# Attention with chunk selection and a gated FFN: in batches 1 to 3, keys, queries with mask columns and attention output transposed by DMA, chunk extremes from a chunk-per-partition load

## The chip, the cores and the metric

The kernel runs on one core of a Trainium2 chip. The metric is the device time of one execution in microseconds (us); lower is better. The result of every run below was compared with the reference. A run counts as slow when it is over 1.5% above the fastest of its kernel. Three runs are slow by this rule, one each of c2_early (382.78 us), c3_all (367.29) and k3 (357.8); medians and ranges below are of fast runs alone. A ratio is the mean time of one kernel's fast runs over the mean time of the other's fast runs in the same rounds on the same chip, with a 95% interval, so it is not quite the ratio of the medians that are quoted beside it.

Engines are named as in the profile: PE is TensorE (matmuls, and transposes done as matmuls against an identity), DVE is VectorE, ACT is ScalarE, POOL is GpSimd, SP is SyncE, which here only issues DMA transfers. Each engine has its own list of instructions. For PE, ACT and DVE a scheduler picks the order of that list when the kernel is built; for POOL and SP, and in the opening, the order is that of the program. In the traces an instruction whose input is late holds back what stands behind it: in the changed kernel (after), DVE stood 2.61 us for a load in front of a reduction (which began at 126.25 us) and SyncE 4.9 us for its input in front of an output transpose (at 258.39), and neither began a later instruction in that time.

## The reference, cut to what matters

```
B, H, S, D = 4, 8, 768, 64;  chunk = 32;  nc = 24;  top_k = 6
k_min, k_max = min and max of each chunk of 32 keys            # "chunk extremes"
ub   = sum over d of max(q * k_min, q * k_max)                 # a bound per query and chunk
ub   = where(chunk is not in the query's future, ub, -1e9)
sel  = the 6 chunks with the largest ub of each query
p    = softmax over keys of (q @ k.T / 8) where sel and causal, else -1e9
x    = (p @ v), heads side by side: 3072 tokens x 512
out  = (sigmoid(x @ w_gate) * (x @ w_val)) @ w_out             # d_ff = 1536
```

## The kernel before

The work is cut into eight units, each half a batch of 384 queries: 0a, 0b, 1a, ... 3b. The first half of a batch is "a" and sees only the first 384 keys, the second is "b" and sees all. After an opening, the kernel runs in stages. A stage holds the attention of one unit, the FFN of the unit before it, the preparation (transposed keys and queries, bounds, picks) of the unit after it, and loads for the unit after that. The matmuls of the three are interleaved, so that PE always has something to do.

The mask costs no instruction of its own: the score matmul contracts over 96 rows, 64 of the head and 32 more. On the key side those 32 rows (of `headK`) hold a fixed pattern with a large negative number where the key lies in that chunk; on the query side (of `headQ`) they hold 1 for each chunk that was not picked.

The parts that change:

```
def keys_t(u, p, pool, tag="ps"):            # PE: three 128x128 transposes of f32 keys, two heads at a time
    ...
    for x in range(HB):
        nc.tensor.transpose(ps[:, x:T:HB], u.k[:, x, 2 * p:2 * p + 2, :].rearrange(...), ident32)
def extremes(u, p):                          # DVE: max and min over each chunk, from the transposed keys
    pv = u.kps[p].rearrange("p (c s) -> p c s", s=CH)
    for e, op in enumerate((ALU.max, ALU.min)):
        nc.vector.tensor_reduce(out=u.kmm[:, p, e, :], in_=pv, op=op, axis=AX.X)
def keys_f(u, p, eng):                       # ACT or DVE: cast to f16 into headK
    for e in range(2):
        eng(headK[u.b % 2][0:64, 2 * p + e, u.rows], ps[64 * e:64 * e + 64])
# queries_t, queries_f: the same for queries.  signs: relu(q), relu(-q), for the bounds
def pick(u, j):                              # bounds back to query rows, sixth largest, "not picked" flags
    ...
    nc.vector.tensor_tensor(apt[j][:, u.sel0:HB, :, 0:cb], ubm, mx[:, :, :, 5:6]..., ALU.is_lt)
def pick_t(u, j, eng):                       # PE: flags transposed; ACT or DVE: into headQ[64:96]
    ...
def turn(u, c):                              # attention output of two heads to xT, which the FFN reads
    ps = ppr.tile([128, T], F16, tag="ps", ...)
    for x in range(HB):
        nc.tensor.transpose(ps[:, 128 * x:128 * x + 128], u.x[:, x, 128 * c:128 * c + 128], ident16)
    nc.vector.tensor_copy(u.xT[:, c, :], ps)
def ffn_gv(u, fb):                           # 12 times a unit
    ... gp = four matmuls of wg16 with u.xT      # "g_" in the profile
    nc.scalar.activation(gate, gp, AF.Tanh, scale=0.5)
    ... vp = four matmuls of wv16 with u.xT      # "v_"
    nc.vector.scalar_tensor_tensor(hg, gate, 1.0, vp, ALU.add, ALU.mult)   # DVE must do this to free gp's and vp's space
```

The softmax here doesn't subtract the row's maximum and nothing guards it: scores larger than these inputs give would overflow.

Of the kernel before, what the change touches and what calls it, by code (L numbers as in the profile page):

```python
# [8 lines left out]
F32 = mybir.dt.float32  # L9
F16 = mybir.dt.float16  # L10
# [8 lines left out]
def kernel(  # L19
# [23 lines left out]
    consts = ctx.enter_context(tc.tile_pool(name="consts", bufs=1))  # L43
    keep = ctx.enter_context(tc.tile_pool(name="keep", bufs=1))
    loads = ctx.enter_context(tc.tile_pool(name="loads", bufs=2))
    nat = ctx.enter_context(tc.tile_pool(name="nat", bufs=1))
    sel = ctx.enter_context(tc.tile_pool(name="sel", bufs=1))
    ubp = ctx.enter_context(tc.tile_pool(name="ubp", bufs=2))
    attp = ctx.enter_context(tc.tile_pool(name="attp", bufs=4))
    small = ctx.enter_context(tc.tile_pool(name="small", bufs=3))  # L50
    xnatp = ctx.enter_context(tc.tile_pool(name="xnatp", bufs=2))
    xtp = ctx.enter_context(tc.tile_pool(name="xtp", bufs=2))
    gatep = ctx.enter_context(tc.tile_pool(name="gatep", bufs=3))
    hglp = ctx.enter_context(tc.tile_pool(name="hglp", bufs=18))
    outp = ctx.enter_context(tc.tile_pool(name="outp", bufs=3))
    PS = bass.MemoryType.PSUM
    pff = ctx.enter_context(tc.tile_pool(name="pff", bufs=3, space=PS))
    psc = ctx.enter_context(tc.tile_pool(name="psc", bufs=3, space=PS))
# [2 lines left out]
    class Unit:  # L61
        def __init__(self, b, half):
            self.b, self.half = b, half
            self.name = f"{b}{'ab'[half]}"
            self.qa, self.qb = HB * half, HB * half + HB
            self.rows = slice(T * half, T * half + T)
            self.sel0 = 1 - half
            self.m = HB - self.sel0
            self.paired = b == 0
            self.cb = T // CH * (half + 1)  # L70
            self.banks = HIGH if half else LOW
            self.where = {}
            base = 0
            for bk in self.banks:
                for (jb, i0, n) in bk:
                    for o in range(0, n, 128):
                        self.where[((i0 + o) // 128, jb)] = base + o
                    base += n
            self.width = base
            self.att, self.pv, self.kps, self.qps, self.ubT = {}, {}, {}, {}, {}  # L80

    LOW = [
# [8 lines left out]
    ]  # L91
    units = [Unit(b, half) for b in range(B) for half in range(2)]

    def load(u):
        for n, src in (("k", k), ("q", q)):
            t = loads.tile([128, H, HB, D], F32, tag="raw" + n, name=f"raw{n}_{u.name}")
            for j in range(2):
                nc.sync.dma_start(t[:, 4 * j:4 * j + 4], src[u.b, 4 * j:4 * j + 4, u.rows].rearrange(  # L98
                    "h (p x) d -> p h x d", x=HB))
            setattr(u, "raw" + n, t)  # L100
        u.v = loads.tile([128, HB, H, D], F32, tag="v", name=f"v_{u.name}")
        for i in range(HB):
            r = T * u.half + 128 * i
            nc.sync.dma_start(u.v[:, i], v[u.b, :, r:r + 128].rearrange("h p d -> p h d"))  # L104

    def regroup(u, n, parts):
        raw = getattr(u, "raw" + n)
        if not hasattr(u, n):
            setattr(u, n, nat.tile([128, HB, H, D], F32, tag=n, name=f"{n}_{u.name}"))
        t = getattr(u, n)  # L110
        for f, h0, h1 in parts:
            f(t[:, :, h0:h1, :], raw[:, h0:h1].rearrange("p h x d -> p x h d"))  # L112
# [3 lines left out]
    epat = consts.tile([32, NC, CH], F16, tag="epat")  # L116
    NQ = 2 * HB - 1
    pen = consts.tile([128, NQ, NC], F32, tag="pen")
    kmx = keep.tile([128, NP, 2, 32], F32, tag="kmx", name="kmx")
    kcat, v16s, apt, headK, headQ = [], [], [], [], []  # L120
    for i in range(2):
        kcat.append(keep.tile([128, H, 32], F32, tag=f"kcat{i}", name=f"kcat{i}"))
        headK.append(keep.tile([96, H, S], F16, tag=f"hk{i}", name=f"hk{i}"))
        headQ.append(keep.tile([96, H, T], F16, tag=f"hq{i}", name=f"hq{i}"))
        apt.append(keep.tile([128, HB, 4, 32], F16, tag=f"ap{i}", name=f"ap{i}"))
        v16s.append(keep.tile([128, 2 * HB, H, D + 1], F16, tag=f"v16{i}", name=f"v16{i}"))

# [4 lines left out]
    def constants():  # L132
        make_identity(nc, ident32)
        nc.vector.memset(epat, 0.0)
        nc.gpsimd.affine_select(
            out=epat, in_=epat, compare_op=ALU.not_equal, fill=NEG,
            base=0, pattern=[[-1, NC], [0, CH]], channel_multiplier=1,
        )
        fill_pattern(0, nc.sync)
        nc.vector.memset(kmx, 0.0)  # L140
        nc.vector.memset(pen, 0.0)
        nc.gpsimd.affine_select(
            out=pen, in_=pen, compare_op=ALU.is_ge, fill=-1e9,
            base=128, pattern=[[128, NQ], [-CH, NC]], channel_multiplier=1,
        )
        for i in range(2):
            nc.vector.memset(kcat[i], 0.0)
            nc.vector.memset(apt[i], 0.0)
            nc.gpsimd.memset(v16s[i][:, :, :, D:D + 1], 1.0)
        nc.vector.memset(headQ[0][64:96, :, 0:128], 0.0)  # L150
        nc.vector.tensor_copy(ident16, ident32)

    wg16 = keep.tile([128, 4, D_FF], F16, tag="wg16")
    wv16 = keep.tile([128, 4, D_FF], F16, tag="wv16")
# [13 lines left out]
    def cast_v(u):  # L168
        nc.gpsimd.tensor_copy(v16s[u.b % 2][:, u.qa:u.qb, :, 0:D], u.v)  # L169
# [63 lines left out]
    def queries_f(u, p, eng):  # L233
        ps = u.qps.pop(p)
        for e in range(2):
            eng(headQ[u.half][0:64, 2 * p + e, :], ps[64 * e:64 * e + 64])  # L236

    def bounds(u, j):
        s0 = 128 * u.sel0
        n = T - s0  # L240
        ps = ppr.tile([128, T], F32, tag="ps", name=f"ubT_{u.name}_{j}")
        for i, e in [(i, e) for e in range(2) for i in range(4)] if u.paired else []:
            h, r = 4 * j + i, 64 * (i % 2)
            nc.tensor.matmul(ps[32 * i:32 * i + 32, 0:n], kmx[r:r + 64, h // 2, e, :],
                             u.qs[r:r + 64, h - h % 2 + e, s0:T], start=(e == 0), stop=(e == 1))
        for i in [] if u.paired else range(4):
            nc.tensor.matmul(ps[32 * i:32 * i + 32, 0:n], kcat[u.b % 2][:, 4 * j + i, :],
                             u.qs[:, 4 * j + i, s0:T], start=True, stop=True)
        t = ubp.tile([128, T], F32, tag="ubT", name=f"ubTs_{u.name}_{j}")
        nc.scalar.copy(t[:, 0:n], ps[:, 0:n])  # L250
        u.ubT[j] = t

    def pick(u, j):
# [10 lines left out]
        for x in range(m):  # L264
            for h in range(4):
                nc.vector.max(mx[:, x, h, :], ubm[:, x, h, :])
        nc.vector.tensor_tensor(apt[j][:, u.sel0:HB, :, 0:cb], ubm,  # L267
                                mx[:, :, :, 5:6].to_broadcast([128, m, 4, cb]), ALU.is_lt)

    def pick_t(u, j, eng):  # L270
        ps = ppr.tile([128, T], F16, tag="ps", name=f"apT_{u.name}_{j}")
# [7 lines left out]
    def score(u, h, x, pool=None, tag="ps"):  # L279
# [6 lines left out]
        o = 0  # L286
        for (jb, i0, w) in u.banks[x]:
            i = i0 - T * u.half
            nc.tensor.matmul(ps[:, o:o + w], headK[u.b % 2][:, h, 128 * jb:128 * jb + 128],  # L289
                             headQ[u.half][:, h, i:i + w], start=True, stop=True)  # L290
            o += w
        nc.scalar.activation(at[:, b0:b0 + n], ps, AF.Exp, scale=scale)  # L292
        if x == 0:
# [4 lines left out]
    def values(u, h):  # L298
        p, e = h // 2, h % 2
        if h == 0:  # L300
            u.x = xnatp.tile([128, HB, H * D], F16, tag="xnat", name=f"xnat_{u.name}")
        if e == 0:
            u.pv[p] = psc.tile([128, 2, HB, D + 1], F32, tag="ps", name=f"pv_{u.name}_{p}")
        at = u.att.pop(h)
# [6 lines left out]
        if e == 1:  # L311
            rz = small.tile([128, 2, HB], F32, tag="rz", name=f"rz_{u.name}_{p}")
            nc.vector.reciprocal(rz, ps[:, :, :, D])  # L313
            o = u.x[:, :, 128 * p:128 * p + 128].rearrange("p a (e d) -> p e a d", e=2)
            nc.vector.tensor_tensor(o, ps[:, :, :, 0:D], rz.unsqueeze(3).to_broadcast([128, 2, HB, D]), ALU.mult)

    def turn(u, c):
        if c == 0:
            u.xT = xtp.tile([128, 4, T], F16, tag="xT", name=f"xT_{u.name}")
        ps = ppr.tile([128, T], F16, tag="ps", name=f"xps_{u.name}_{c}")  # L320
        for x in range(HB):
            nc.tensor.transpose(ps[:, 128 * x:128 * x + 128], u.x[:, x, 128 * c:128 * c + 128], ident16)
        nc.vector.tensor_copy(u.xT[:, c, :], ps)

    hgl = {}
# [29 lines left out]

    A, V, G = nc.scalar.copy, nc.vector.tensor_copy, nc.gpsimd.tensor_copy

    def prep_tasks(u):
        even = [A, V, A, V] if u.half == 0 else [A, A, A, V]
        kf = [V, V, V, V] if u.half == 0 else [A, A, A, A]  # L360
        qf = [A, V, A, V]
# [16 lines left out]
    def opening(u, w):  # L378
# [77 lines left out]
        cast_v(w)  # L456
        for j in range(3):
            load_wo(j)
        fill_pattern(1, nc.sync)
        f = ffn_tasks(u)  # L460

        def more():
            f.pop(0)[1]()
# [73 lines left out]

    with tc.manual_schedule():
        prev = opening(units[0], units[1])
    load(units[2])  # L540
    for i in range(1, len(units)):
        u = units[i]
        prep = prep_tasks(units[i + 1]) if i + 1 < len(units) else []
        a = attend_tasks(u, prep)
        if i + 2 < len(units):
            a.insert(len(a) // 2, (0.0, lambda i=i: load(units[i + 2])))
        merge(a, prev)
        prev = ffn_tasks(u)
    for c, t in prev:
# [31 lines left out]
```

## Time and profile before

The first runs gave 357.35 us, median of 3 (355.92 to 360.1). The page of the profile, its heading, its part 1 (busy us, share of the span, instructions) and two rows of its part 2 (the span in 40 slices: clock granted to PE and mean DMA busy share, in tenths, 9 is 90% or more):

```profile
span 353.9 us, 7200 instructions
PE 316.5 (89%) x2736; PEld 197.0 (56%) x2736; DVE 216.4 (61%) x642; ACT 234.4 (66%) x501; POOL 74.1 (21%) x106
...
PEclk9979999999999999999999999999999999999999
DMA  8999992057900066001740039001100020001002
```

The DMA engines are 80% busy or more in the first 53 us (six slices of 8.8 us) and more than half idle on average after that. The stages, in the windows view of before (columns: window and length in us, then busy us and instruction count of PE, PEld, DVE, ACT and POOL, the clock granted, the DMA share, GB/s):

```profile
87.00:129.00 42.00, 38.91 (x318) 23.26 (x316) 27.59 (x86) 32.05 (x71) 9.63 (x13) 1.00 0.31 83
129.00:171.00 42.00, 39.90 (x387) 25.77 (x386) 28.82 (x84) 29.47 (x64) 7.74 (x12) 1.00 0.29 76
171.00:211.00 40.00, 36.82 (x296) 22.39 (x297) 26.95 (x80) 29.14 (x63) 9.27 (x12) 1.00 0.31 81
```

So PE works 37 to 40 of every 40 to 42 us: the middle stages are bound by the amount of work on PE, and DVE is idle for a third of the time. PE's waits are small. The longest ones, in the waits view of before (engine, instruction and its line, what it waited for; us in total, times, longest us):

```profile
PE kT_0a_172 L179 <- DVE k_0a L112: 4.9, 1, 4.9
PE v_0b_1593 L336 <- ACT gate_0b_1559 L333: 1.4, 1, 1.4
```

The first is in the opening, before there is anything to do. From then on nothing costs more than 1.4 us. The chunk extremes are short instructions on the 384 columns of one pair of heads, as a line of the groups view of before shows (busy us, mean ns of one | idle before and releaser):

```profile
L186 DVE TENSOR_REDUCE kmm_2a<-kT_2a_1933 128x12 f32<-128x384 f32 x2 | 1.1, 553 | 1.0 <-PE kT_2a_1933 L179 1.0
```

| before | us |
|---|---|
| span of the profiled execution | 353.9 |
| PE busy | 316.5 |
| PE not busy (span less busy) | 37.4 |
| DVE / ACT busy | 216.4 / 234.4 |
| the first 55 us, in which PE was busy 37 | 55 |

### The profile page before, as it was taken

The numbers are of one execution on the slowest core, as the hardware profiler recorded it, in microseconds if no ns is written. First come the engines' busy times: TensorE is split into PE (matmuls) and PEld (weight loads), VectorE is DVE, ScalarE is ACT, GpSimd is POOL, SyncE is SP. The second block draws the span as 40 slices with busy tenths as digits, with TensorE's granted clock in tenths as the row PEclk, the third lists the DMA queues.
The fourth block names the chain that finished last, engine by engine and source line by source line (L and its number), as shares of the span: only waits on it lengthen the run. The fifth ranks groups of instructions, "written<-read, shape, count | busy, mean of one in ns | idle before, by whom it ended". The sixth has DMA issues, their size and how long they took to land.

```text
span 353.9 us, 7200 instructions
## 1 busy us (share of the span) xinstructions
PE 316.5 (89%) x2736; PEld 197.0 (56%) x2736; DVE 216.4 (61%) x642; ACT 234.4 (66%) x501; POOL 74.1 (21%) x106
## 2 busy tenths in 40 slices
PE   4678687999988999999987999999998999999995
PEld 3265345656554566655664466665665456665552
DVE  6576548985667569864776469883585574322430
ACT  4683467787888475876789375884789467665321
POOL 3393204211420040210421032201421011110000
PEclk9979999999999999999999999999999999999999
DMA  8999992057900066001740039001100020001002
GB/s 223 268 207 224 232 226 49 0 163 198 267 3 0 31 199 130 2 0 62 222 77 0 32 113 215 3 0 52 41 0 2 0 87 4 2 3 59 31 0 89
DMA packets 50642, 31.13 MB, mean 88 GB/s; under 512 B 26032, under 2 KB 47536, under 8 KB 50608
## 3 DMA queue, kind: packets, MB, share of 16 engines
q1 hardware_dynamic: 45856, 25.96, 28.2%
q0 software_dynamic: 4752, 4.72, 7.8%
q8 instruction: 21, 0.34, 0.4%
q14 instruction: 13, 0.11, 0.1%
HBM read 28.31 MB, written 6.29 MB: 98 GB/s over the span
## 4 chain that ended last, share of the span: by engine, by line
PE 54%; ACT 16%; issue 10%; DVE 8%; DMA 5%; SPq 4%; POOL 2%; ACTq 0%; POOLq 0%; DVEq 0%
DMA v_0b<-in_v_dram 5%; SPq L104 2%; ACT hq_117 L236 2%; SPq L98 1%; ACT hq_112 L236 1%; ACT qs_2b L227 1%; ACT qs_3b L227 1%; ACT qs_1b L227 1%; ACT hk_116 L198 1%; PE o_2b_4225 L345 1%; PE o_1b_2989 L345 1%; PE o_1a_2399 L345 1%; ACT qs_1a L227 1%; PE o_2a_3645 L345 1%; PE o_0b_1743 L345 1%
## 5 line engine op out<-in xcount | busy, mean ns | idle before, releaser
L336 PEld LDWEIGHTS <-wv_121 128*128 128x128 f16 x384 | 37.0, 97 | 38.4 <-issue 16.6
L330 PEld LDWEIGHTS <-wg_120 128*128 128x128 f16 x384 | 35.2, 98 | 16.1 <-issue 1.9
L289 PEld LDWEIGHTS <-hk_111 96*128 96x128 f16 x240 | 19.7, 101 | 13.0 <-issue 8.2
L289 PEld LDWEIGHTS <-hk_116 96*128 96x128 f16 x240 | 19.2, 97 | 9.4 <-issue 3.1
L179 PE MATMUL kT_0a_172<-ident_105,k_0a 128*128 128x128 f32 x3 | 0.9, 430 | 4.9 <-DVE k_0a L112 4.9
L295 POOL TENSOR_SCALAR_AFFINE_SELECT att_0b_776<-att_0b_776 128x384 f16<-128x384 f16 x1 | 0.5, 515 | 19.7 <-ACT att_0b_776 L292 19.7
L179 PEld LDWEIGHTS kT_0a_172<-ident_105,k_0a 128*128 128x128 f32 x3 | 0.5, 213 | 4.8 <-issue 4.8
L277 ACT COPY hq_117<-apT_0b_735 32x384 f16<-32x384 f16 x4 | 1.9, 469 | 1.8 <-PE apT_0b_735 L273 1.8
L112 ACT COPY k_0a<-rawk_0a 128x384 f32<-128x384 f32 x2 | 1.0, 512 | 2.9 <-DMA rawk_0a<-in_k_dram 2.9
L192 DVE TENSOR_SCALAR kcat_110<-kmm_2b 64x24 f32<-64x24 f32 x8 | 2.8, 350 | 0.1
L192 DVE TENSOR_SCALAR kcat_115<-kmm_3b 64x24 f32<-64x24 f32 x8 | 2.8, 350 | 0.1
L313 DVE RECIPROCAL rz_3b_4888<-pv_3b_4849 128x6 f32<-128x6 f32 x1 | 0.2, 196 | 4.3 <-PE pv_3b_4849 L309 4.3
L277 DVE COPY hq_112<-apT_3a_3801 32x256 f16<-32x256 f16 x4 | 1.2, 288 | 2.7 <-PE apT_3a_3801 L273 2.7
L277 DVE COPY hq_112<-apT_2a_2555 32x256 f16<-32x256 f16 x4 | 1.2, 288 | 2.7 <-PE apT_2a_2555 L273 2.7
L169 POOL CAST v_114<-v_0b 128x1536 f16<-128x1536 f32 x1 | 1.5, 1465 | 6.1 <-DMA v_0b<-in_v_dram 6.1
L313 DVE RECIPROCAL rz_1b_2434<-pv_1b_2339 128x6 f32<-128x6 f32 x1 | 0.2, 196 | 4.0 <-PE pv_1b_2339 L309 4.0
L313 DVE RECIPROCAL rz_2b_3680<-pv_2b_3585 128x6 f32<-128x6 f32 x1 | 0.2, 197 | 4.0 <-PE pv_2b_3585 L309 4.0
L273 PEld LDWEIGHTS <-ap_118 128*128 128x128 f16 x20 | 1.7, 98 | 1.5 <-DVE ap_118 L267 0.2
L162 POOL DMA_DIRECT2D wg_120<-in_moe_w_gate_dram x3 | 2.4, 808 | 0.0
L348 ACT ACTIVATE osb_3b_5093<-o_3b_5080 128x512 f32<-128x512 f32 x1 | 0.6, 597 | 2.8 <-PE o_3b_5080 L345 2.8
L198 ACT CAST hk_111<-kT_0b_494 64x384 f16<-64x384 f32 x2 | 0.9, 474 | 2.2 <-DVE kmx L186 2.2
L169 POOL CAST v_114<-v_0a 128x1536 f16<-128x1536 f32 x1 | 1.5, 1469 | 4.4 <-DMA v_0a<-in_v_dram 4.4
(1976 smaller groups left out, 1085.3 us busy)
## 6 DMA issues: line engine op xcount, KB each, us to landing
wg_120<-in_moe_w_gate_dram POOLq DMA_DIRECT2D x3, 512.0 KB, 8.9
wv_121<-in_moe_w_val_dram POOLq DMA_DIRECT2D x3, 512.0 KB, 12.0
wo_122<-in_moe_w_out_dram POOLq DMA_DIRECT2D x3, 512.0 KB, 13.6
rawk_0a<-in_k_dram SPq DMA_DIRECT2D x2, 384.0 KB, 3.8
rawq_0a<-in_q_dram SPq DMA_DIRECT2D x2, 384.0 KB, 5.2
v_0a<-in_v_dram SPq DMA_DIRECT2D x3, 256.0 KB, 6.3
rawk_0b<-in_k_dram SPq DMA_DIRECT2D x2, 384.0 KB, 6.3
rawq_0b<-in_q_dram SPq DMA_DIRECT2D x2, 384.0 KB, 6.5
```

The source lines that it names most:

```text
L98: nc.sync.dma_start(t[:, 4 * j:4 * j + 4], src[u.b, 4 * j:4 * j + 4, u.rows].rearrange("h (p x) d -> p h x d", x=HB))
L104: nc.sync.dma_start(u.v[:, i], v[u.b, :, r:r + 128].rearrange("h p d -> p h d"))
L169: nc.gpsimd.tensor_copy(v16s[u.b % 2][:, u.qa:u.qb, :, 0:D], u.v)
L192: nc.vector.tensor_scalar_mul(kcat[u.b % 2][64 * i:64 * i + 64, 4 * j + e:4 * j + 4:2, c0:c0 + T // CH], u.kmm[64 * e:64 * e + 64, 2 * j:2 ...
L198: eng(headK[u.b % 2][0:64, 2 * p + e, u.rows], ps[64 * e:64 * e + 64])
L227: nc.scalar.activation(o, src, AF.Relu, scale=sign)
L236: eng(headQ[u.half][0:64, 2 * p + e, :], ps[64 * e:64 * e + 64])
L277: eng(headQ[u.half][64:96, 4 * j + i, s0:T], ps[32 * i:32 * i + 32, s0:T])
L289: nc.tensor.matmul(ps[:, o:o + w], headK[u.b % 2][:, h, 128 * jb:128 * jb + 128], headQ[u.half][:, h, i:i + w], start=True, stop=True)
L330: nc.tensor.matmul(gp, wg16[:, c, 128 * fb:128 * fb + 128], u.xT[:, c, :], start=(c == 0), stop=(c == 3))
L336: nc.tensor.matmul(vp, wv16[:, c, 128 * fb:128 * fb + 128], u.xT[:, c, :], start=(c == 0), stop=(c == 3))
L345: nc.tensor.matmul(op, hgl[(u.name, fc)][:, 128 * tb:128 * tb + 128], wo16[:, fc, :], start=(fc == 0), stop=(fc == NFB - 1))
```

## The change

The intent is to take layout work off PE, ACT and DVE, and to give it to DMA engines that are half idle. For batches 1 to 3 ("wide" units), POOL casts keys and queries to f16, and transfers that are transposed on their way write them (`dma_start_transpose`, in the profile DMA_TRANSPOSE): keys together with their pattern rows (3 transfers of 256 KB a unit), queries together with their mask columns (6 of 128 KB), attention output (4 of 96 KB). Chunk extremes need f32 keys with a chunk's 32 keys in one partition's row, so the keys of a batch are loaded a second time in that shape (two loads of 768 KB) and DVE reduces over them; a reduction now covers 96 chunks (four heads) and 32 of the 64 head columns. A few buffers are taken away to make room. The diff, cut to its core:

```diff
-    attp = ... bufs=4      hglp = ... bufs=18     outp = ... bufs=3     v in `loads`, bufs=2
+    attp = ... bufs=3      hglp = ... bufs=15     outp = ... bufs=2     v in `loadv`, bufs=1
+            self.wide = b > 0
+    def load_span(u, j):                       # the second load of the keys
+        t = kcp.tile([96, CH, D], F32, tag="kc", ...)                       # bufs=1
+        nc.sync.dma_start(t, k[u.b, 4 * j:4 * j + 4].rearrange("h (c s) d -> (h c) s d", s=CH))
+    def keys_wide(u):
+        nc.gpsimd.tensor_copy(kn16[u.half][:, :, :, 0:D], u.k)
+        for x in range(HB):
+            r = T * u.half + 128 * x
+            nc.sync.dma_start_transpose(headK[u.b % 2][:, :, r:r + 128],
+                                        kn16[u.half][:, x].rearrange("p h c -> p (h c)"))
+    def span_reduce(u, j, e):
+        src = u.kc[j].rearrange("p s d -> p d s")
+        for d0 in (0, 32):
+            nc.vector.tensor_reduce(out=u.kmm[:, e, d0:d0 + 32], in_=src[:, d0:d0 + 32],
+                                    op=(ALU.max, ALU.min)[e], axis=AX.X)
+    def span_t(u, j):                          # one PE transpose of 96 columns, for four heads
+        nc.tensor.transpose(ps, u.kmm..., ident32[0:96, 0:96])
+    def queries_wide(u):
+        nc.gpsimd.tensor_copy(qn16[:, :, :, 0:D], u.q)
+        if u.sel0: ... first_rows(u, 0)        # the first 128 queries need no picks
+    def send_rows(u, j, x):
+        nc.sync.dma_start_transpose(headQ[u.half][:, 4 * j:4 * j + 4, 128 * x:128 * x + 128],
+                                    qn16[:, x, 4 * j:4 * j + 4].rearrange("p h c -> p (h c)"))
     def pick(u, j):
-        nc.vector.tensor_tensor(apt[j][:, u.sel0:HB, :, 0:cb], ubm,
+        dst = qn16[:, u.sel0:HB, 4 * j:4 * j + 4, 64:64 + cb] if u.wide else apt[j][...]
+        nc.vector.tensor_tensor(dst, ubm,
+        if u.wide:
+            for x in range(u.sel0, HB):
+                send_rows(u, j, x)
     def turn(u, c):
+        if u is not units[0] and not (u is units[-1] and c == 3):
+            nc.sync.dma_start_transpose(u.xT[:, c, :].rearrange("p (x i) -> p x i", x=HB),
+                                        u.x[:, c].rearrange("p x d -> p (x d)"))
+            return
... (prep_wide orders these tasks; loads of a later unit are spread over the stage;
     one fill of the key pattern is dropped from the opening)
```

Queries are still transposed on PE in f32 for the bounds, and their positive and negative parts are still made by ACT.

## The prediction

It was made before the changed kernel ran, and is quoted word for word, apart from two passages that are cut, with the cuts marked: a time for one transpose by DMA that no run of this case had measured, and the reason for the upper end of the range, which rested on a speed of the transposes that no trace had shown. The sum: 357 - 15 - 8 + 13 - 2 = 345 us. Two figures in it are estimates and more loosely based than the rest: 1.1 us for a reduction of 1024 elements (0.55 us for 384 columns would in proportion give 1.47), and 3 us of queue for the second key load, for which no measured number is given. The 18 and 14 us of queue are estimates from the 2.05 us that a v load of 256 KB occupied it for in before.

> **What bounds the kernel now.** The page: span 353.9 us, PE busy 316.5 (89%), ACT 234.4 (66%), DVE 216.4 (61%), POOL 74.1. The windows view splits it: the opening (0 to 55 us) is a chain of loads and small steps with PE busy 37 of 55; from 55 us each half batch is a stage of about 40 us, with PE busy 38.9 of 42 (87 to 129), 39.9 of 42 (129 to 171), 36.8 of 40 (171 to 211), DVE 27 to 29 and ACT 29 to 32. The chain of waits is 54% PE, 16% ACT, 8% DVE. So six middle stages are bound by PE's own work, with 2 to 3 us of scattered idle behind ACT (waits of 0.5 to 1.4 us).
>
> **What the change removes, per stage of batches 1 to 3.**
> - PE: 12 key transposes (start to start about 0.11 us, not the 0.27 us of one record), 4 query transposes in the first half only, 4 to 6 mask and 12 output transposes at about 0.055 us: 2.6 us together, 15 over six stages.
> - ACT, over all six: 24 key casts and 24 query casts of 0.474 us, 24 mask copies of 0.36 or 0.47 us, against 12 more sign activations of 0.376: net about 28 us.
> - DVE: 48 extremes of 0.55, 48 chunk scalings, 48 casts of 0.55, 24 mask copies, 27 output copies of 0.35; it gains 24 reductions of 96x1024 elements, near 1.1 us (estimate from 0.55 for 384 columns). Net about 55 us less.
>
> **What it adds.** All on the SyncE queue: per stage 3 key transposes of 256 KB, 4 to 6 query ones of 128 KB, 4 output ones of 96 KB, key and query loads cut to 256-byte pieces (v: 256 KB each, queue occupied about 2.05 us each in steady state, 6 to 7.5 us to landing), and every batch's keys a second time (1.5 MB). Loads are then about 9 x 2 = 18 us per stage plus some 3 for the second key load; if a transposed 256 KB costs like a 256 KB v load, transposes add about 14: an estimated 35 of 40 us of queue. [...] Latency is exposed at stage ends: the last picks come about 6 us before the next scores, and two batches of mask transposes plus the last output transpose queue behind each other. I expect 2 to 3 us of PE idle per boundary, waiting for query or output transposes. The opening loses one pattern fill.
>
> **Sum.** -15 us PE work, about -8 us of idle behind ACT and DVE, +13 us new waits, about -2 us in the opening: 345 us. Range 326 to 378 [...]. Faster by over 2%: 0.57; within: 0.22; slower: 0.21.
>
> **What would show it.** PE busy about 300 us or less; ACT near 205, DVE near 160; DMA share in the middle slices up from 0.3 towards 0.7 or more; key, query-mask and output transposes landing in 3 to 6 us; first PE waits of each stage naming DMA transposes; stages of 37 to 39 us.
>
> **What would make it wrong.** Transposes that take 6 us or more each, or SyncE held by a waiting transpose so that loads and output stores come late; DVE standing at the second key load.

## More of the kernel before

PE is busy 89% of the time, and its clock is full from the fourth slice on.

`gp` and `vp` live in three shared buffers of PE's accumulator memory. If DVE does not consume them, PE runs out of buffers after a block and a half.

## The result, and the profile after

The changed kernel took 402.04 us, median of 4 runs (400.39 to 404.97), against 357.26 us (355.92 to 360.1) for the kernel before in the same rounds. The ratio is 1.125 (1.1151 to 1.1349): slower by an eighth. The result is correct. The page of after, the same lines:

```profile
span 398.7 us, 6796 instructions
PE 324.7 (81%) x2547; PEld 195.7 (49%) x2547; DVE 180.3 (45%) x472; ACT 207.9 (52%) x441; POOL 79.5 (20%) x116
...
PEclk9867999996889696979978999696999999899999
DMA  8999990598439846796255956494437015001002
```

PE has 189 instructions fewer and is busy 8 us longer. ACT has lost 27 us and DVE 36 us, as intended. Neither helped. The new thing is the clock row: in the middle of the run it drops to 6 to 8 tenths again and again. The windows view of after:

```profile
154.00:202.00 48.00, 42.28 (x366) 26.57 (x364) 21.22 (x52) 28.24 (x62) 7.47 (x12) 0.89 0.67 124
202.00:247.00 45.00, 36.81 (x276) 21.55 (x277) 22.39 (x56) 22.83 (x49) 10.29 (x14) 0.92 0.70 132
247.00:298.00 51.00, 42.00 (x347) 25.79 (x347) 21.22 (x52) 27.13 (x59) 7.08 (x12) 0.87 0.57 119
298.00:335.00 37.00, 33.68 (x274) 20.44 (x271) 15.35 (x52) 22.08 (x49) 8.07 (x12) 1.00 0.37 73
```

The first two windows do the work of the last two shown of before: 48 us in place of 42, and 45 in place of 40. The DMA share more than doubled, and is still 0.3 or more short of full. The last window (the attention of 3a) is the only one of the four at full clock, and it takes 37 us; no extremes are prepared in it, and few transfers are left (DMA share 0.37). This is what the change gives where nothing stands still for long.

PE's waits, in the waits view of after:

```profile
PE xps_0a L415 <- DVE xT_0a L416: 5.9, 1, 5.9
PE kmT_1a L295 <- DVE kmm_1a L290: 5.2, 1, 5.2
...
PE v_0b L429 <- DVE hg_0b L432: 4.0, 1, 4.0
PE g_1b L423 <- DMA xT_1b<-xnat_1b: 3.9, 1, 3.9
PE g_2a L423 <- DMA xT_2a<-xnat_2a: 3.6, 1, 3.6
...
PE g_3a L423 <- DMA xT_3a<-xnat_3a: 3.1, 1, 3.1
```

The long ones are of two kinds. One ends with DVE: extremes (kmm), output copies and gates (hg) that come late. The other ends with a DMA: the transposed attention output (xT, 12.1 us in sum) and, in shorter pieces, the transposed queries (hq, 7.2 us). Summed over the whole waits view, PE waits 31.7 us for DVE (9.8 in before), 15.8 for ACT (22.1 in before) and 19.3 for DMA transfers (none in before).

**The first kind.** The groups view of after shows the reductions, and the timeline of DVE shows what one batch of them does:

```profile
L290 DVE TENSOR_REDUCE kmm_2a<-kc_2a 96x32 f32<-96x1024 f32 x8 | 14.8, 1866 | 4.5 <-DMA kc_2a<-in_k_dram 4.5
```

```profile
126.25 1.88 DVE L290 TENSOR_REDUCE kmm_2a<-kc_2a 96x32 f32<-96x1024 f32 x1 [2.61 <-DMA kc_2a<-in_k_dram]
128.06 0.18 DVE L402 RECIPROCAL rz_1a<-pv_1a 128x6 f32<-128x6 f32 x1
128.16 1.81 DVE L290 TENSOR_REDUCE kmm_2a<-kc_2a 96x32 f32<-96x1024 f32 x1
129.90 0.54 DVE L404 TENSOR_TENSOR xnat_1a<-pv_1a,rz_1a 128x384 f16<-128x384 f32 x1
130.36 1.00 DVE L432 SCALAR_TENSOR_TENSOR hg_0b<-gate_0b,v_0b 128x384 f16<-128x384 f16 x2
```

The columns of a timeline are start, length, engine, line, operation, tiles, and in brackets the idle time before it and its releaser. DVE stood 2.61 us for the second load of the keys, then did two reductions of 1.8 to 1.9 us, and reached the gates (hg_0b) only at 130.36. By then PE had used up its buffers: the wait of 4.0 us for hg_0b in the list above ends at 130.95. DVE is 45% busy, but what it does is in the way of what PE needs.

**The second kind.** The timeline of SyncE's queue in after, around the wait of g_2a:

```profile
238.53 3.81 SPq L311 DMA_TRANSPOSE hq<-qn  x3
242.44 0.53 SPq L443 DMA_DIRECT2D out_dram<-osb_1b  x1
243.08 3.84 SPq L311 DMA_TRANSPOSE hq<-qn  x3
247.01 1.00 SPq L443 DMA_DIRECT2D out_dram<-osb_1b  x1
248.11 1.20 SPq L410 DMA_TRANSPOSE xT_2a<-xnat_2a  x1
```

and DVE's and PE's timelines at the same place, the output tile that the last transpose reads, and the first matmul that waits for it:

```profile
242.43 0.56 DVE L404 TENSOR_TENSOR xnat_2a<-pv_2a,rz_2a 128x384 f16<-128x384 f32 x1
...
250.46 0.48 PE L423 MATMUL g_2a<-xT_2a,wg 128*128 128x384 f16 x1 [3.56 <-DMA xT_2a<-xnat_2a]
```

The output was ready at 242.99 (242.43 + 0.56) and its transpose was issued at 248.11, 5.1 us later, and the matmul started 2.35 us after that. In between SyncE was occupied by three query transposes of 1.28 us each and a store of 1.0 us. The number of bytes hardly matters for this time: in the whole run the median occupation of SyncE was 1.20 us for 96 KB, 1.26 us for 128 KB and 1.33 us for 256 KB (9 of the 81 took 1.6 to 2.8), against 0.33 us for the shortest store of an output block. The times to landing, in the list of DMA issues of after (queue, kind, count, KB each where they are given, median us from issue to landing), were all short:

```profile
rawk_2a<-in_k_dram SPq DMA_DIRECT2D x3, 256.0 KB, 8.0
rawq_2a<-in_q_dram SPq DMA_DIRECT2D x3, 256.0 KB, 4.6
...
hq<-qn SPq DMA_TRANSPOSE x36, 2.5
...
hk<-kn SPq DMA_TRANSPOSE x18, 3.3
```

A transposed 256 KB (hk) landed in 3.3 us, plain loads of 256 KB in 4.6 (rawq_2a) and 8.0 (rawk_2a). In this trace no group of transposes landed later in the median (3.4 us at most, xT_0b) than such a load (4.1 us at least, rawq_3b). It is no test of transposing alone, since the loads read DRAM tensors (in_k_dram, in_q_dram) and the transposes read tiles.

SyncE also stood still at output transposes whose input was not ready: 4.0 us before 214.30 and 4.9 us before 258.39. The second key load was issued right behind each (215.5 and 259.6). This was a danger that the prediction had named. It is not what made DVE wait for these loads, though: in a3_turn_pe below, which has no such transposes, DVE still stood for them, 4.6 us for kc_2a and 7.1 for kc_3a (4.5 and 4.1 in after).

**The clock.** After a wait PE does not go on as before. The windows view of after, around the wait of 3.9 us for xT_1b, in steps of 2 us:

```profile
204.00:206.00 2.00, 0.00 (x0) 0.00 (x0) 0.00 (x0) 0.34 (x1) 2.00 (x3) 0.81 0.26 49
206.00:208.00 2.00, 0.51 (x2) 0.25 (x2) 0.00 (x0) 0.00 (x0) 1.31 (x2) 0.50 0.32 64
...
210.00:212.00 2.00, 2.00 (x7) 0.88 (x6) 0.56 (x1) 1.02 (x3) 0.00 (x0) 0.50 0.72 139
212.00:214.00 2.00, 2.00 (x18) 1.28 (x17) 0.99 (x3) 1.24 (x3) 0.52 (x1) 0.98 0.00 0
```

PE is idle from 203.6 to 207.5. From 206 to 212 it has half its clock. At half clock it gets 7 instructions done from 210 to 212, at full clock 18 from 212 to 214. The mean of 0.81 from 204 to 206 puts the fall at about 205.2, only 1.6 us after PE had stopped, and windows of 0.5 us put the rise at 212.1: 6.8 us at half clock, about 4.5 us of them with work. In such windows after has twelve stretches at half clock, ten of 6.8 us and two of 3.4 (14.1 to 17.5 and 338.4 to 341.8 us), 75 us in all; before has one of 6.8 us in the opening (21.5 to 28.3) and half clock in its last 1.3 us, after PE's last matmul. Elsewhere in after the clock fell after single waits of 2.6 us (one ends at 173.8, the other at 269.5). A wait of this size was not always enough: in q1_merge, below, waits of 2.6 and 2.1 us between 254 and 260 left the clock full. What else decides it is not shown.

**The sum.** The difference in span can be split exactly, by definition, into three: idle time of PE (span less busy time), time lost to the lower clock, and the rest, PE's work at full clock. The second is an estimate from the trace: for each window of 1 us, PE's busy time times the missing part of the clock. It assumes that all of PE's work slows with the clock.

| us, profiled executions | before | after | difference |
|---|---|---|---|
| span | 353.9 | 398.7 | +44.8 |
| PE not busy | 37.4 | 73.9 | +36.5 |
| lost to half clock | 3.2 | 29.7 | +26.5 |
| PE work at full clock | 313.3 | 295.1 | -18.2 |

This is bookkeeping. It says where PE's time is, and not yet what caused it.

### The profile page after: what moved, and what is told of

It reads as the page before. It is cut to its first block, busy times and chain, and to the rows that moved or that the text cites. A ratio compares the mean times of both kernels' runs of the same rounds, so it can differ in the third digit from the quotient of the medians.

```text
span 398.7 us, 6796 instructions
## 1 busy us (share of the span) xinstructions
PE 324.7 (81%) x2547; PEld 195.7 (49%) x2547; DVE 180.3 (45%) x472; ACT 207.9 (52%) x441; POOL 79.5 (20%) x116
## 5 line engine op out<-in xcount | busy, mean ns | idle before, releaser
L429 PEld LDWEIGHTS <-wv 128*128 128x128 f16 x384 | 39.9, 104 | 55.8 <-issue 34.9
L378 PEld LDWEIGHTS <-hk 96*128 96x128 f16 x480 | 41.3, 105 | 33.5 <-issue 23.2
L423 PEld LDWEIGHTS <-wg 128*128 128x128 f16 x384 | 37.1, 103 | 25.8 <-issue 12.4
L381 ACT ACTIVATE att_1b<-sc_1b 128x512 f16<-128x512 f32 (+1 forms) x32 | 16.9, 574 | 7.4 <-PE sc_1b L378 7.2
L381 ACT ACTIVATE att_2b<-sc_2b 128x512 f16<-128x512 f32 (+1 forms) x32 | 16.8, 574 | 4.7 <-PE sc_2b L378 4.5
L381 ACT ACTIVATE att_3b<-sc_3b 128x512 f16<-128x512 f32 (+1 forms) x32 | 16.6, 570 | 5.0 <-PE sc_3b L378 4.7
L381 ACT ACTIVATE att_0b<-sc_0b 128x512 f16<-128x512 f32 (+1 forms) x32 | 16.6, 573 | 2.7 <-PE sc_0b L378 2.3
L290 DVE TENSOR_REDUCE kmm_1a<-kc_1a 96x32 f32<-96x1024 f32 x8 | 14.6, 1864 | 6.2 <-DMA kc_1a<-in_k_dram 6.2
L290 DVE TENSOR_REDUCE kmm_3a<-kc_3a 96x32 f32<-96x1024 f32 x8 | 14.9, 1887 | 4.1 <-DMA kc_3a<-in_k_dram 4.1
L290 DVE TENSOR_REDUCE kmm_2a<-kc_2a 96x32 f32<-96x1024 f32 x8 | 14.8, 1866 | 4.5 <-DMA kc_2a<-in_k_dram 4.5
L423 PE MATMUL g_1b<-xT_1b,wg 128*128 128x384 f16 x48 | 11.3, 349 | 3.9 <-DMA xT_1b<-xnat_1b 3.9
## 6 DMA issues: line engine op xcount, KB each, us to landing
wv<-in_moe_w_val_dram POOLq DMA_DIRECT2D x3, 512.0 KB, 14.1
```

Source lines behind the costliest of these rows:

```text
L290: nc.vector.tensor_reduce(out=u.kmm[:, e, d0:d0 + 32], in_=src[:, d0:d0 + 32], op=(ALU.max, ALU.min)[e], axis=AX.X)
L378: nc.tensor.matmul(ps[:, o:o + w], headK[u.b % 2][0:96, h, 128 * jb:128 * jb + 128], headQ[u.half][0:96, h, i:i + w], start=True, stop=True)
L381: nc.scalar.activation(at[:, b0:b0 + n], ps, AF.Exp, scale=scale)
L423: nc.tensor.matmul(gp, wg16[:, c, 128 * fb:128 * fb + 128], u.xT[:, c, :], start=(c == 0), stop=(c == 3))
L429: nc.tensor.matmul(vp, wv16[:, c, 128 * fb:128 * fb + 128], u.xT[:, c, :], start=(c == 0), stop=(c == 3))
```

## The experiments

The theories have letters in the expectations. D: DVE is blocked by the long reductions. T: the latency of DMA transposes is exposed at the ends of stages. B: the smaller pools cost the time. Then, after the first four runs, Q: each transpose occupies SyncE's queue for about 1.2 us, and the one that is wanted waits behind others, against L: the latency of the transfer itself. Later O: batch 1 is prepared in the opening, where DMA is full (0.8 busy or more). C: it is the clock after idle stretches that costs. Fifteen kernels ran, in four groups; the kernel before had medians of 358.63, 356.64, 356.31 and 356.78 us in these groups. Gains over after are differences of medians from different groups, so taken to be good to some 2 us, and only large ones are used. The scheduler makes a new order for each variant, so no edit moves only one thing.

### First group: what is the bound?

**a1_copy**: reductions replaced by a copy of the first key of each chunk. It gives a wrong result (relative error 0.53); all other instructions stay.

```diff
-        src = u.kc[j].rearrange("p s d -> p d s")
-        for d0 in (0, 32):
-            nc.vector.tensor_reduce(out=u.kmm[:, e, d0:d0 + 32], in_=src[:, d0:d0 + 32], op=..., axis=AX.X)
+        nc.vector.tensor_copy(u.kmm[:, e, :], u.kc[j][:, 0, :])
```

> Changed kernel with the 24 chunk reductions replaced by copies of each chunk's first key (wrong result on purpose; loads, transposes and order kept as far as the scheduler allows). Theory D (VectorE blocked by the reductions, four of 1.86 us in a row, behind which PE starves and its clock falls): six gaps of 3 to 7 us at the reductions go, with the half-clock stretches after them; about 402 to 365 us, mean clock from 0.906 to about 0.95. Theory T [...]: at most 12 us faster, gaps at 105, 150, 205, 250, 298 and 337 us stay.

Measured: 379.08 us (375.93 to 381.47), ratio 1.0565 (1.0487 to 1.0643); DVE busy 140.6 us. The gain is 23 us of the 37 that D had been given, where the reductions had taken 44.3 us of DVE (14.6 + 14.8 + 14.9). D holds in kind and is not the whole: waits for the transposed output stayed (4.1 us for xT_1b, 4.3 for xT_2a, 3.1 for xT_3a).

**a3_turn_pe**: the attention output back on PE and DVE.

```diff
-        if u is not units[0] and not (u is units[-1] and c == 3):
+        if False:
```

> Changed kernel with all attention output transposed on PE again, keys and queries still by DMA. Theory T: the 12 us of PE waits on output transposes at stage starts go, with some half-clock time after them: 402 to about 385 us. Theory D: under 6 us change.

Measured: 388.89 us (386.5 to 391.06), ratio 1.0843 (1.077 to 1.0915), 13 us less than after, though 81 PE transposes and their copies came back. That is near what T had been given (385), and more than D alone allows. No wait for xT is left, apart from that of unit 0a in the opening. The longest ones after the opening are now for DVE: 4.8 us (kmm_1a), 3.6 (hg_1b), 2.8 (hg_1a), 2.7 (kmm_2a).

**a4_qpe**: queries and mask columns back on PE, ACT and DVE; keys and output stay on DMA.

```diff
-        dst = qn16[:, u.sel0:HB, 4 * j:4 * j + 4, 64:64 + cb] if u.wide else apt[j][:, u.sel0:HB, :, 0:cb]
+        dst = apt[j][:, u.sel0:HB, :, 0:cb]
-        if u.wide:
-            for x in range(u.sel0, HB): send_rows(u, j, x)
     (prep_wide: queries_f and pick_t again, queries_wide taken out)
```

> Changed kernel with query and mask rows transposed on PE and copied by ACT and DVE again; keys and output still by DMA, reductions as in the changed kernel. Theory T: PE waits on query transposes (about 6 us by the wait list) go, but 30 us of ACT and DVE copies return: 395 to 405 us. Theory D: the reductions still block, no gain: 400 to 410 us.

Measured: 378.75 us (375.55 to 380.42), ratio 1.0542 (1.046 to 1.0625), 23 us less than after, much more than either expectation. The waits for the output transposes went with the query transposes, all but one of 1.4 us and three below 1 us, although the output transposes themselves were still there. If PE had waited for the latency of those transfers alone, the waits would have stayed. This led to theory Q and to the reading of SyncE's timeline that is shown above.

**b1_buffers**: the kernel before with the smaller pools (attention tiles 3, gate products 15, output 2).

> Kernel before with the smaller pools of the change alone (attention tiles 4 to 3, gated products 18 to 15, output tiles 3 to 2). Theory B (the smaller pools cost the time): 370 us or more. Theories D and T: within 1.5% of 357 us.

Measured: 356.4 us (355.79 to 356.83), ratio 0.9937 (0.9892 to 0.9982). The smaller pools cost nothing, and B falls (the single buffer for v was not in this run).

### Second group: earlier, shorter, and both

**c2_early**: preparation tasks are spread 1.4 times as densely, so that picks and their transposes come earlier in the stage.

```diff
-        per = len(prep) / (H * nb)
+        per = 1.4 * len(prep) / (H * nb)
```

> Changed kernel, preparation of the next half batch issued 1.4 times as fast, so that the picks end at about 70% of the stage instead of its end. Theory T (latency at stage ends): PE's waits on query transposes (6 us) vanish and half-clock time after them too: 402 to about 390 us. Theory D (reductions block VectorE): no less than 398, the six reduction gaps stay, and preparation that comes earlier may stand in front of the previous half's gates.

Measured: 379.36 us, median of 3 fast runs (376.56 to 380.1), ratio 1.0598 (1.0527 to 1.0669). Waits for the query transposes are gone; of those for output transposes 4.3, 2.2, 3.2 and 3.1 us remain. Still a gain of 23 us, more than T was given (390), and D alone had forbidden it. PE's waits for gates (hg) fell too, from 11.3 us in sum to 5.4, so earlier preparation shortens both kinds of wait and does not tell them apart.

**c5_dve_tree**: extremes by pairwise maximum and minimum over rows that lie side by side, in five steps.

```diff
-            nc.vector.tensor_reduce(...)      # two strided reductions
+        op, t = (ALU.max, ALU.min)[e], u.kc[j]          # for e == 0: t is scratch of 96 x 16 x 64
+        for r in (0, 8):
+            nc.vector.tensor_tensor(t[:, r:r + 8], u.kc[j][:, r:r + 8], u.kc[j][:, 16 + r:24 + r], op)
+        for n in (8, 4, 2):
+            nc.vector.tensor_tensor(t[:, 0:n], t[:, 0:n], t[:, n:2 * n], op)
+        nc.vector.tensor_tensor(u.kmm[:, e, :], t[:, 0, :], t[:, 1, :], op)
```

> Changed kernel, each chunk extreme computed by pairwise maxima and minima of contiguous rows instead of a reduction over a strided axis: 12 instructions for four, no piece above 512 columns. Theory D with stride as the cause of 1.86 us for 1024 elements: about 5 us instead of 7.4 us per batch half of heads, no instruction above 0.65 us, 402 to about 385 us. If the length of the block does not matter, only 6 x 2.4 us of VectorE work goes and the time is 395 or more.

Measured: 377.49 us (377.25 to 382.84), ratio 1.0611 (1.0515 to 1.0708), correct. DVE is busy 168.4 us against 180.3, and the block is made of pieces of 0.84 us at most in a group's mean (a single one took 1.00; the 0.65 that was expected, like the 5 us, was the author's estimate), between which the scheduler can put gates. The longest group, in the groups view of this run:

```profile
L293 DVE TENSOR_TENSOR tree_2a<-kc_2a 96x512 f32<-96x512 f32 x4 | 3.2, 838 | 2.4 <-DMA kc_2a<-in_k_dram 2.0 <-PE ubT_1b L337 0.4
```

It got the gain of a1_copy (25 against 23 us), with 12 us less on DVE and not 40. So it is the length of the block in front of the gates that counts, more than DVE's total.

**c3_all**: the tree, the earlier preparation, and the last quarter of each output back on PE (`c != 3` in the condition of `turn`).

> Changed kernel with three repairs: pairwise extremes, earlier picks, and the last quarter of each attention output transposed on PE. Theories D and T together: both sorts of gap go and the clock stays near 0.97, so that PE's smaller work shows: 350 to 365 us. If a third cause remains (reordered queue, ACT bunching its sign activations): above 370.

Measured: 362.08 us, median of 3 fast runs (360.87 to 364.85), ratio 1.0149 (1.0076 to 1.0221), verdict unclear; a gain of 40 of the 45 us. Waits for xT of 4.8, 3.6 and 3.2 us remained, with the output transposes still behind query transposes in SyncE's queue, and the last output block of unit 0a was stored at 100.0 us, against 86.8 in before.

**c4_keys_only**: only the keys by DMA and the tree; queries, masks and output on PE.

> Only keys by DMA transpose and extremes from the chunk-per-partition load (pairwise): queries, masks and attention output on PE as before the change. Theory T is then out of play: 355 to 365 us if D's blocks are cured by the pairwise form; above 370 if the extremes' load and VectorE time still hold PE.

Measured: 363.07 us (362.01 to 364.22), ratio 1.0162 (1.0113 to 1.0212), verdict unclear. As good as c3_all with much less moved.

### Third group: the queue, the opening, the stride

**q1_merge**: after with the query and mask transposes of four heads joined into one transfer (18 query transposes in place of 36), by a changed layout of `qn16` and `headQ`.

```diff
-            for x in range(u.sel0, HB):
-                send_rows(u, j, x)
+            send_rows(u, j, u.sel0, HB)       # headQ[..][:, j, x:y] <- qn16[:, j, x:y], up to 384 KB in one
```

> Changed kernel, the two or three query and mask transposes of four heads joined into one transfer of the same bytes (layouts of the query tiles rearranged for it). Theory Q (the 1.2 us that each transpose occupies SyncE's in-order queue, whatever its bytes, holds the output transpose behind it up to 5 us at stage ends): occupied time per four heads from 3.8 to about 1.5 us, the 3 to 4 us waits of PE on output transposes fall below 1.5 us, 402 to about 388 us. Theory L (the latency of the transfer itself, 2.3 us or more, is what PE waits for): waits unchanged, 398 to 404 us.

Measured: 383.19 us (380.21 to 385.04), ratio 1.0731 (1.0659 to 1.0804), 19 us less than after. The timeline of SyncE's queue at the end of the same stage:

```profile
232.14 1.43 SPq L315 DMA_TRANSPOSE hq<-qn  x1
233.66 0.84 SPq L447 DMA_DIRECT2D out_dram<-osb_1b  x1
234.59 1.21 SPq L414 DMA_TRANSPOSE xT_2a<-xnat_2a  x1
```

A joined transpose of three times the bytes holds SyncE for 1.43 us here (median of all joined and single ones 1.30), where three had held it for 3.8. It lands later (median 3.7 us against 2.5), and the waits for output transposes fell all the same, from 12.1 us in sum (3.9 + 3.6 + 3.1 + 1.5) to 5.0 (2.5 + 1.8 + 0.7). If latency had been the matter they would have grown. Q holds against L, though 2.5 and 1.8 us are more than the 1.5 that Q had been given. Most of the gain came by way of the clock: by the bookkeeping above, PE's idle time in this run is 69.6 us (73.9 in after, and the opening alone has a wait of 10.2 in place of 5.9), and the loss to half clock is 13.5 us in place of 29.7.

**k0_late**: keys and queries of batch 1 as in before; only batches 2 and 3 are wide. The attention output of 0b and of batch 1 still goes by DMA (the condition in `turn` does not ask for `wide`).

```diff
-            self.wide = b > 0
+            self.wide = b > 1
```

> The change applied to batches 2 and 3 alone; batch 1 on PE as before the change (with its second pattern fill). Theory O (much of the loss is that batch 1's second key load and blocks fall into the opening, where the weights fill the DMA queues): the first output block of the first half batch back at 87 us instead of 100, half of the loss or more gone: 375 to 380 us. If each stage loses alike, a third goes: about 387 us.

Measured: 378.3 us (376.85 to 381.18), ratio 1.0629 (1.0555 to 1.0703), 24 us less than after. The last output block of unit 0a is stored at 85.5 us (before 86.8, after 100.6), so O is shown as to the place: 13.8 us of the loss were there already at 100 us, and they go when batch 1's keys and queries stay on PE. That full DMA is the reason, and not something else of batch 1, is argued from the following, not isolated. In after the second key load of 1a has a median of 9.6 us to landing, against 5.8 later, DVE stands for it (6.2 us), and copies and gates of unit 0a stand behind DVE. Batch 1 is also a third of the wide preparation, so not all of the 24 us belong to the opening.

**d1_contig** (one look, wrong on purpose, relative error 0.498): the reductions run over 32 neighbouring elements in place of 32 that are 256 bytes apart.

```diff
-        src = u.kc[j].rearrange("p s d -> p d s")
+        src = u.kc[j].rearrange("p s d -> p (s d)").rearrange("p (a b) -> p a b", b=CH)
```

> Changed kernel with the reductions over 32 neighbouring elements instead of 32 elements 256 bytes apart (wrong result on purpose, same count). If the stride makes 1.86 us of 1024 elements: about 1.1 to 1.2 us each, and 402 to about 390 us. If not: 1.8 us or more, and no change of time.

Measured: one time of 385.12 us, of unknown state, so only the duration is used. The group in this run, to be set against the 1866 ns shown of after:

```profile
L290 DVE TENSOR_REDUCE kmm_2a<-kc_2a 96x32 f32<-96x1024 f32 x8 | 9.5, 1204 | 4.5 <-DMA kc_2a<-in_k_dram 4.5
```

The stride alone (nothing else in the instruction changed) makes the same reduction 1.55 times as long (1866 / 1204). What makes the stride cost this much was not tested.

**k1_best**: q1_merge, k0_late, the tree, earlier preparation and the last output quarter on PE, together.

> All repairs together: change for batches 2 and 3 alone, pairwise extremes, joined query transposes, earlier picks, last quarter of each attention output on PE. If theories D, Q and O name the whole loss, PE's smaller work shows at last: 345 to 355 us, faster than before by 1 to 3%. If not, 357 to 365 us.

Measured: 355.72 us (353.16 to 357.67), ratio 0.9965 (0.9898 to 1.0032): level with before, and just above the range expected. All of the loss is gone, in part because the change itself is taken back for batch 1.

### Fourth group: the clock, and the best version

**w1_warm**: 40 small matmuls put in front of the fourth matmul of the first gate block, to keep PE's clock up while it waits for the output transpose.

```diff
         for c in range(4):
+            if c == 3 and fb == 0 and u is not units[0] and u is not units[-1]:
+                for _ in range(40):
+                    nc.tensor.matmul(vp[:, 0:96], ident16, ident16[:, 0:96], start=True, stop=True)
     (vp's buffer is now taken before gp's matmuls, in every block, not after the gate)
```

> Changed kernel with 40 extra matmuls (128x128x96, result overwritten) placed in PE's order just before the fourth gate matmul of a half batch, the one that waits up to 3.9 us for the last output transpose. Theory C (half clock after an idle stretch costs as much as the idle stretch): PE does not fall to half clock after these waits, mean clock up from 0.906 by 0.02 to 0.03, 402 to about 391 us although PE gets some 15 us more to do. If only the idle time counts: 402 to 410 us, since nothing is waited for less.

Measured: 410.15 us (407.88 to 413.33), ratio 1.1488 (1.1424 to 1.1553). It did not test what it was made for. The filler lasted only 1.9 us (47 ns each; some 11 us over six half batches, where 15 was the estimate), the waits behind it were still 2.0 to 4.4 us, the clock in the mean of the run was 0.913 (after 0.906), and other waits were longer (10.2 us in the opening, 5.9 in after; 6.0 for hg_0b, 4.0 in after). The earlier claim on vp's buffer may have a part in this; it was not separated. Inconclusive: C as a cause by itself stays open.

**k3**: as k1_best, with the earlier preparation only while a wide unit is being prepared.

```diff
-        per = 1.4 * len(prep) / (H * nb)
+        per = (1.0 if u.b == 0 or (u.b == 1 and u.half == 0) else 1.4) * len(prep) / (H * nb)
```

> As k1_best, but only the preparation of DMA-transposed half batches is hurried, by 1.4; batch 1 keeps the pace of the kernel before. If the 4 us that k1_best lost against before in the first two stages came from the hurry: about 351 us, 1 to 2% faster than before. If not: 355 us again.

Measured: 353.01 us, median of 5 fast runs (350.72 to 355.75), against 356.78 us, median of 11 (355.86 to 359.54); ratio 0.9885 (0.9835 to 0.9934), correct. This is 1.1% faster than before, the lowest median of all kernels here. The windows view of k3, stages whose outputs are those of 1b, 2a and 2b:

```profile
175.00:209.00 34.00, 32.74 (x261) 19.44 (x260) 20.53 (x66) 20.71 (x47) 8.62 (x12) 1.00 0.83 171
209.00:253.00 44.00, 40.45 (x361) 24.54 (x360) 19.10 (x60) 28.07 (x62) 8.82 (x13) 0.96 0.66 134
253.00:287.00 34.00, 32.76 (x267) 19.71 (x264) 16.27 (x55) 20.73 (x46) 8.47 (x12) 1.00 0.35 79
```

Measured from one unit's last store to the next, these stages took 39.4, 42.4 and 39.4 us in before. So the first and the last became 34 us and gained what the idea promised, more than 5 us each. The first of them even holds half of the extremes of batch 3 (the pieces run from 195.5 to 205.2 us, and DVE waits for no load there), so extremes as such do not cost the time. The stage between, with the other half of them, takes 44 us and gains nothing: DVE stands 3.6 us for the second load of batch 3's keys, and PE waits 2.1 us for DVE's gate product (hg_2a). In the stage before these, which has the second half of batch 2's extremes, PE waits 3.0 us for them (kmm_2a). The DMA share of 0.83 in the fastest stage also shows that DMA bandwidth is not what held after back. Nor is it the cut of key and query loads to 256-byte pieces, which no run tried alone: k3 keeps it for batches 2 and 3.

**k4**: as k3 with all output transposes on PE and a density of 1.2.

> As k3 with all attention output on PE and the hurry at 1.2. Theory Q: SyncE's queue keeps only key and joined query transposes, so no output waits remain, but PE gets 0.5 us and VectorE 1 us more per stage: 350 to 355 us.

Measured: 354.47 us (351.55 to 354.99), ratio 0.9905 (0.9846 to 0.9964). Level with k3: once the query transposes are joined, output by DMA or by PE makes no difference that these runs show (the 0.5 and 1 us a stage in the expectation are estimates from nine PE transposes of 0.055 us and three copies of 0.35 us in before; the density changed with it, so the two are not separated).

## Why the prediction was wrong

The prediction said 345 us with 326 to 378, and faster as the likeliest. It was 402.04 us and slower by an eighth. Point by point:

- **"-15 us PE work": right.** At full clock PE lost 18.2 us of work, by the estimate above. ACT at 207.9 us (205 predicted) and a DMA share of 0.57 to 0.70 in the middle stages (0.7 predicted) were right too. "PE busy about 300 us or less" was not: 324.7, because the same work ran in part at half clock.
- **Transposes "landing in 3 to 6 us": better than predicted**, 2.3 us (output), 2.5 (queries) and 3.3 (keys). The prediction's main worry, transposes so slow that the queue is the bound, did not come true. The upper end of the range was drawn for that danger, and so missed the real ones.
- **"24 reductions of 96x1024 elements, near 1.1 us": failed.** They took 1.86 us. The author's estimate, below what proportion gives (1.47), started from a reduction of 384 columns (0.55 us) that lay in the accumulator memory with neighbouring elements. 1.20 us is what neighbouring elements cost here (d1_contig), close to the estimate; the stride made the difference.
- **DVE counted as a sum of busy time ("net about 55 us less"): failed.** DVE did come down, by 36 us (the longer reductions, 24 x 0.76 = 18 us, are nearly all that is missing), and the kernel did not gain from it. Four reductions in a row (4 x 1.86 = 7.4 us when nothing is put between them) and the wait for the second key load stand in front of gates that PE needs. a1_copy and c5_dve_tree took 23 and 25 us off, the latter with only 12 us less on DVE. The prediction had named "DVE standing at the second key load" among what could go wrong, and gave it no us.
- **"If a transposed 256 KB costs like a 256 KB v load" and "2 to 3 us of PE idle per boundary": mis-sized.** The queue was costed by bytes. What each transpose takes from SyncE is about 1.2 to 1.3 us whatever its size (medians of after, 96 to 256 KB), so the six small query transposes of a unit cost nearly as much as six large ones, and the output transpose that PE waits for stood 5.1 us behind three of them and a store. The waits for output transposes were 3.9, 3.6, 1.5 and 3.1 us, and 7.2 us for query transposes came on top: 19.3 us in place of 13. q1_merge shows the cause: the same bytes in half as many transfers, and the waits fell from 12.1 to 5.0 us.
- **"+13 us new waits, about -8 us of idle behind ACT and DVE": this step failed most.** Idle time of PE grew by 36.5 us, not by a net 5. The waits for transposes were 19.3 us and those behind ACT fell by 6.3, both of the kind that was forecast. But the waits behind DVE did not fall: they grew by 21.9 us (9.8 to 31.7), for the reasons of the two points above. The prediction had this term with the wrong sign.
- **The clock: missing from the sum.** Nothing in the prediction stood for the half clock after an idle stretch; the trace puts 26.5 us there. In before, waits after the opening are 1.4 us at most and the clock does not drop until PE's work is done (PE stops at 350.0 us, the clock falls at 352.6). Waits of 2.6 us and more changed that. How much would come back if the waits stayed and the clock did not fall is not shown by an experiment; w1_warm failed to show it.
- **"About -2 us in the opening": wrong in sign.** The last output block of unit 0a came 13.8 us later. Batch 1's loads, second key load and transposes fell into the time when the DMA share is 0.8 or more, and k0_late, which leaves batch 1's keys and queries on PE, brought it back to 85.5 us.
- **"Stages of 37 to 39 us": 48, 45, 51 and 37.** The last one is the prediction's stage, at full clock; the others are what waits and half clock made of it.

What stays open: the gains of the single edits (13 to 25 us each) sum to far more than 45 us, since each shortens waits that also bring the clock down and since each reorders the engines; k1_best, which joins the query transposes, spares batch 1, has the tree, prepares earlier and puts one output quarter back, shows that together they remove the whole loss (in part by taking the change back for batch 1 and a quarter of the output), but not each one's share.

## What to carry to other kernels

Before moving work from a bound engine to DMA, count not only bytes and latency but the time each transfer occupies the engine that issues it (medians of 1.20 to 1.33 us for a transpose in after, from 96 to 256 KB), and look at what stands behind it in that queue: join small transfers (q1_merge took 19 us off), and let the one that the bound engine waits for go first (xT_2a stood 5.1 us behind others). An engine that is half idle can still starve the bound one (DVE, 45% busy in after, kept PE waiting for 31.7 us), if long instructions or a wait stand in front of the short ones that free the bound engine's buffers; cut long blocks into pieces (c5_dve_tree took 25 us off). Count an idle stretch of PE with what may follow it: in after every single wait of 2.6 us or more that came later than the opening was followed by 3.4 or 6.8 us at half clock (in q1_merge waits of 2.6 and 2.1 us were not), and 26.5 us of lost clock came with 36.5 us more of idle time. Keep new transfers out of an opening in which DMA is already full (0.8 busy or more here; k0_late took 24 us off, not all of it in the opening).
